# A second z buffer for the inverse transform, one piece of it to a slot, and a new order of work in the slots

## The chip, the cores and the metric

One core of a Trainium2 chip. The time is that of one execution on the device, in microseconds; lower is better. TensorE (PE) multiplies, ScalarE (ACT) and VectorE (DVE) empty its accumulators (PSUM) and do the elementwise work, GpSimd (POOL) issues some transfers, and the sync engine (SP) the others.

## What is computed

Eight sequences of 2496 rows of 256 numbers go through a spectral layer and then, row by row, through a mixture of eight experts with one expert to a row:

```python
X = np.fft.rfft(x, axis=1)
Yr = Xr @ w_r - Xi @ w_i + b_r
Yi = Xr @ w_i + Xi @ w_r + b_i
Yr = np.sign(Yr) * np.maximum(np.abs(Yr) - lam, 0.0)     # lam = 0.01, the same for Yi
y = np.fft.irfft(Y, n=x.shape[1], axis=1)
...
expert_idx = np.argmax(logits, axis=1)                    # logits = y @ w_gate, probs = softmax
for e in range(E):
    xe = y[mask]                                          # mask = expert_idx == e
    out[mask] = gate_w[mask, None] * (np.maximum(xe @ w1[e], 0.0) @ w2[e])
```

## The kernel before

The program has two long stages. The **spectral stage** handles eight batches (b) in ten slots (s) each, 80 slots in all; slot number `it` is 10 b + s. The **expert stage** multiplies 82 tiles of rows, sorted by expert, with the experts' weights.

Both transforms are done in two steps, as matmuls with fixed matrices. In the names of the program, which the profile shows too:

- `fwd_a` (matmul `pa`, copy `ae`) is the first step of the forward transform, for the next batch; its result goes to a buffer in DRAM (`spec`) and comes back transposed (`turn`, tile `t`).
- `fwd_b` (`pb`) is the second step, for the next slot. `halves` takes its result apart for a product in two parts: ScalarE copies `re` and `sh`, VectorE computes `su` and two `sl`.
- `mix` multiplies with the layer's weights: `pk` (copied to `k` by ScalarE) and `pm`, which VectorE adds to `k` as `v`.
- `shrink` is the soft threshold: `r` on ScalarE, four `y` on VectorE.
- `inv_b` (`pv`) is the first step of the inverse transform. ScalarE copies the result into the one large tile `z`, which holds a whole batch.
- `inv_a` is the second step. It needs the whole of `z`, and goes in twelve pieces: a piece has four matmuls `pz`, after each pair of which ScalarE rounds to `zh` and VectorE takes the rest `zl`, and six matmuls `py` on the `zh` and `zl` of the piece before, copied to `yb` by ScalarE.
- `route` is a generator that finds expert, gate and place of the finished rows: some 25 small steps, nearly all on VectorE (`lg`, `mx`, `scan`, `carry`, `carry_b`, `rb`), and the small matmuls `pr`. `tick(n)` takes n steps of the routes that are under way. `table` writes the list of tiles in the same manner, driven by `nudge`.

The order of the instructions on TensorE, ScalarE, VectorE and SP is that of the code; nothing reorders them. Tiles come from pools with a number of buffers; whoever takes a buffer again waits until its last reader is done. The accumulator tags are `u` (four buffers, for pa, pz, pv), `yo` (two, for pk, py and pr), and one buffer each for pb and pm.

Before the change there is one z. While batch b − 1 is taken out of it, slots of batch b cannot write to it, so their `inv_b` is put off: the twelve pieces stand in slots 2 to 5 of the next batch, three to a slot (`turning`), and the ten `inv_b` behind them, two to a slot from slot 6 on. After the last slot come the last two `inv_b` with eight warming matmuls (`keep_warm(8)`, `pw`) between them, the pieces of the last batch (`finish_last`), and the expert tiles, into whose first tiles the last routes' steps are laid by `breathe`.

Of the kernel before, what the change touches and what calls it, by code (L numbers as in the profile page):

```python
# [10 lines left out]
F32 = mybir.dt.float32  # L11
# [89 lines left out]
class Kernel:  # L101
    def __init__(self, tc, nb, x, w_r, w_i, b_r, b_i, w_gate, w1, w2,
                 c_fa, c_fe, c_ga, c_bm, c_bi, c_ids, c_score, c_base, c_ltri, c_tcol, out):
        self.__dict__.update({n: v for n, v in locals().items() if n != "self"})
        self.nc = tc.nc
        self.ntok = nb * S
        self.cap = TT + self.ntok
        self.nt = (self.ntok + E * (TT - 1)) // TT
        assert (nb - 3) * S - E * (TT - 1) > (EARLY - 1) * TT
        self.early = EARLY  # L110
        self.spec = [self.nc.dram_tensor(f"spec{i}_dram", (120, G, D), F32, kind="Internal").ap() for i in range(2)]
        self.xs = self.nc.dram_tensor("xs_dram", (E * self.cap, XW), F32, kind="Internal").ap()
# [24 lines left out]
    def open_inverse(self, st, pst):  # L137
# [34 lines left out]
        self.mark = k.tile([1, 1], F32, name="mark")  # L172
        self.z = k.tile([128, 2, 66, 40], F32, name="z")

    def open_forward(self, st):
        tc, nc, nb = self.tc, self.nc, self.nb
        f = self.f = self.pool(st, "f", 1, side="right")
        self.xst = ExitStack()
        self.xp = self.pool(self.xst, "xp", 5)
        self.tp = self.pool(st, "tp", 6, side="right")  # L180
# [15 lines left out]
        self.raw = {}  # L196
        self.braw = self.w.tile([33, 2, D], F32, tag="y", name="braw", bufs=6)
        for h, b in ((0, self.b_r), (1, self.b_i)):
# [12 lines left out]
        nc.gpsimd.dma_start(self.tcol, self.c_tcol)  # L211
        nc.gpsimd.memset(self.z[:, :, 64:66, :], 0.0)

# [38 lines left out]
    def split_bias(self):  # L252
        nc = self.nc
        zero = self.w.tile([128, 2, D], F32, tag="y", name="zero", bufs=6)
        nc.vector.memset(zero, 0.0)
        nc.vector.tensor_copy(self.bias, zero)
        nc.vector.tensor_scalar_add(self.ones, zero[:, 0, 0:128], 1.0)
        bh = self.w.tile([33, 2, D], F32R, tag="y", name="bh", bufs=6)
        nc.scalar.copy(self.bias[0:1], self.braw[0:1])
        nc.scalar.copy(bh[32:33], self.braw[32:33])  # L260
        nc.vector.tensor_sub(self.bias[32:33], self.braw[32:33], bh[32:33])
# [18 lines left out]
    def fwd_a(self, b, q, g):  # L280
# [4 lines left out]
                         self.xg[b, q][:m, g:g + 2, :].rearrange("p g d -> p (g d)"), start=True, stop=True)  # L285
        ae = self.xp.tile([120, 2, D], F32, tag="ae", name="ae", bufs=8)
        to = ae.rearrange("p g d -> p (g d)")
# [67 lines left out]
    def shrink(self, b, s):  # L355
# [4 lines left out]
        yield  # L360
        y = self.w.tile([128, 2, D], F32, tag="y", name="y", bufs=6)
        for kp in range(2):
# [8 lines left out]
    def inv_b(self, b, s):  # L371
        nc = self.nc
        y = self.ys.pop((b, s))
        p = self.psi.tile([128, 512], F32, tag="u", name="pv", bufs=4).rearrange(
            "p (c a r n) -> p c a r n", c=2, a=2, r=2)
        for kp in range(2):
            for c in range(2):
                nc.tensor.matmul(p[:, c, kp, :, :], y[:, kp, c * 128:(c + 1) * 128], self.bi[:, 2 * s + kp, :],  # L378
                                 start=True, stop=True)
        for c in range(2):  # L380
            nc.scalar.copy(self.z[:, c, 0:NB, 4 * s:4 * s + 4].rearrange("p n a -> p a n"),  # L381
                           p[:, c].rearrange("p a r n -> p (a r) n"))

    def inv_a(self, b, i):
        nc = self.nc
        for g in (2 * i, 2 * i + 1) if i < GH else ():
            p = self.psi.tile([128, 512], F32, tag="u", name="pz", bufs=4)
            for c in range(2):
                nc.tensor.matmul(p[:120, c * 136:(c + 1) * 136],  # L389
                                 self.z[:, c, 3 * g:3 * g + 3, :].rearrange("p j a -> p (j a)"), self.iw[:, c, :],  # L390
                                 start=True, stop=True)
# [16 lines left out]
    def spectral(self, fwd):  # L408
# [39 lines left out]
        for b in range(nb):  # L448
            for s in range(10):
                o = s + 2 if b == 0 or s > 7 else 6 + s // 2  # L450
                if 10 * b + o < n:
                    back[10 * b + o].append((b, s))

        for it in range(n):
            b, s = todo[it]
            half, small = iter(()), iter(())
            turning = b and 2 <= s < 6
            if it + 1 < n:
                self.fwd_b(*todo[it + 1])
                half = self.halves(*todo[it + 1])  # L460
                next(half)
            turns = iter(range(3 * s - 6, 3 * s - 3) if turning else ())

            def inverse():
                if back[it]:
                    self.inv_b(*back[it].pop(0))
                for i in turns:
                    self.inv_a(b - 1, i)
                    break

            if turning:
                inverse()
            if it:
                small = self.shrink(*todo[it - 1])
                next(small)
            next(half, None)
            self.tick(2)
            self.nudge(it)
            if not turning:
                inverse()  # L480
            mix = self.mix(b, s)
            if not turning:
                next(mix)
            for a in first[it]:
                self.fwd_a(*a)
            if turning:
                next(mix)
            next(small, None)
            self.tick(2)
            self.nudge(it)  # L490
            inverse()
            next(small, None)
            if it:
                self.pace(self.ys[todo[it - 1]][0:1, 1, 0:1])
                self.send(1)
            self.tick(1)
            next(mix, None)
            inverse()
            self.tick(1)
            self.pace(self.us[b, s][0:1, 0, 0:1])  # L500
            self.send(1)
            for a in loads[it]:
# [5 lines left out]
            if it + 4 < n:  # L508
                self.turn(*todo[it + 4])
            if b == nb - 2 and s == 1:  # L510
                self.tabling = self.table(0)
            if b == nb - 1 and s == 5:
                self.open_early()
        for _ in self.shrink(*todo[n - 1]):
            pass
        self.inv_b(*todo[n - 2])
        self.pace(self.ys[todo[n - 1]][0:1, 1, 0:1])
        self.send(1)
        self.keep_warm(8)
        self.inv_b(*todo[n - 1])  # L520
        self.pace(self.z[0:1, 1, 0, 36:37])
        self.send(1)
        fwd.close()

# [16 lines left out]

    def nudge(self, it=0):
        for _ in range(2 if it % 10 < 7 else 0):
            if next(self.tabling, "wait") == "wait":
                break

    def breathe(self):
        self.tick(3)
        self.nudge()

    def finish_last(self):
        tiles = itertools.chain.from_iterable(self.step(t) for t in range(BUSY))
        fill = itertools.chain(self.first1(), self.first2())
        for i in range(GH + 1):
            self.inv_a(self.nb - 1, i)
            if i:
                self.pace(self.yb[0:1, (2 * i - 1) % GH, 8:9])
                self.send(1)
            else:
                for _ in self.upright(0):  # L560
# [16 lines left out]
    def route(self, b, hf, y):  # L577
# [42 lines left out]
        nc.vector.tensor_copy(sb, pa[:, GH - 1, :])  # L620
        for _ in range(8 if b >= self.nb - 3 else 4):
            yield
# [388 lines left out]
```

## Time and profile before

| | |
|---|---|
| median of 3 runs | 1548.9 us (1548.7 to 1549.89) |
| profiled execution | 1556.04 us |
| its span, first to last instruction | 1554.3 us |
| TensorE busy | 1516.7 us, 98% |
| VectorE, ScalarE, GpSimd busy | 59%, 50%, 25% |

Busy times are those that the profiler records, and the ends of matmuls are modelled: a matmul's record is longer than the step to the next one. So 98% says that TensorE rarely has nothing to do, not that its array is at its peak. A matmul with fp32 operands is recorded as two. Starts are exact enough to measure steps between groups of matmuls, and a bracket at the end of a row of the timeline gives the engine's idle time before it and what ended it.

### The profile page before, as it was taken

What the parts mean: (1) busy time and instruction counts of PE and PEld (TensorE: products, weight loads), DVE (VectorE), ACT (ScalarE), POOL (GpSimd) and SP (SyncE); (2) the same over time, 40 slices, a digit from 0 to 9 for tenths busy, and PEclk for the clock granted to TensorE, in tenths of its full rate; (3) what the DMA queues carried; (4) which work ended last, traced back from release to release, by engine and by line L of the source; (5) the groups of instructions that cost most, each with busy time, mean ns of one, the idle gap of its engine ahead of it and who ended that gap; (6) DMA issues with size and microseconds to landing.
All of it is one profiled execution on the core that took longest, in us unless ns stands there. A gap on an engine that the chain in (4) does not pass through costs nothing. (4 is left out here: it accounts for less than half of the span.)

```text
span 1554.3 us, 35598 instructions
## 1 busy us (share of the span) xinstructions
PE 1516.7 (98%) x10934; PEld 1398.6 (90%) x10934; DVE 912.2 (59%) x2102; ACT 782.2 (50%) x1689; POOL 394.8 (25%) x554
## 2 busy tenths in 40 slices
PE   6999999999999999999999999999999999999997
PEld 3899999998989888889999999999999999999996
DVE  3677787777778777655455545545445445445442
ACT  2667777777767666344344434434334334334332
POOL 1002433425151534334311111111112111111111
PEclk7999999999999999999999999999999999999998
DMA  8864554646353422334234332323213213132210
GB/s 238 231 193 115 174 145 136 179 119 195 111 172 94 147 58 61 84 91 121 65 100 106 95 77 72 97 52 94 56 42 98 49 47 103 42 78 69 49 42 21
DMA packets 192834, 159.94 MB, mean 103 GB/s; under 512 B 127770, under 2 KB 163264, under 8 KB 192365
## 3 DMA queue, kind: packets, MB, share of 16 engines
q1 hardware_dynamic: 172685, 113.43, 28.8%
q0 software_dynamic: 19936, 44.04, 8.5%
q8 instruction: 89, 1.46, 0.4%
q14 instruction: 124, 1.02, 0.2%
HBM read 241.99 MB, written 66.37 MB: 198 GB/s over the span
## 5 line engine op out<-in xcount | busy, mean ns | idle before, releaser
L939 PE MATMUL po<-h,hh 128*128 128x512 f32 x1312 | 462.1, 395 | 0.0
L902 PE MATMUL ph<-xh,h 128*128 128x256 f32 x1312 | 372.0, 284 | 1.8 <-DVE hl L908 1.8
L902 PE MATMUL ph<-xl,h 128*128 128x256 f32 x1312 | 371.1, 283 | 0.0
L902 PE MATMUL ph<-xh,l 128*128 128x256 f32 x1312 | 370.7, 283 | 0.0
L936 PE MATMUL po<-h,hl 128*128 128x256 f32 x1148 | 324.0, 282 | 0.2 <-DVE hl L908 0.2
L908 DVE SCALAR_TENSOR_TENSOR hl<-ph,hh 128x512 fp32r<-128x512 f32 x328 | 226.2, 690 | 149.3 <-ACT hh L907 114.2
L907 ACT ACTIVATE hh<-ph 128x512 fp32r<-128x512 f32 x328 | 193.8, 597 | 204.0 <-PE ph L902 198.4
L939 PEld LDWEIGHTS po<-h,hh 128*128 128x128 f32 x1312 | 241.5, 188 | 43.8 <-issue 0.2
L948 POOL DMA_INDIRECT out<-o,row x124 | 123.8, 998 | 581.1 <-DVE o L946 472.7
L902 PEld LDWEIGHTS ph<-xh,l 128*128 128x128 f32 x1312 | 251.0, 191 | 3.7
L902 PEld LDWEIGHTS ph<-xh,h 128*128 128x128 f32 x1312 | 251.0, 191 | 3.2 <-DVE hl L908 3.2
L946 DVE SCALAR_TENSOR_TENSOR o<-po,xr,part 128x256 f32<-128x256 f32 x156 | 75.4, 484 | 302.6 <-ACTq L864 153.7
L902 PEld LDWEIGHTS ph<-xl,h 128*128 128x128 f32 x1312 | 251.1, 191 | 0.0
L945 ACT ACTIVATE part<-po,xr 128x256 f32<-128x256 f32 x156 | 73.8, 473 | 334.1 <-PE po L939 324.9
L936 PEld LDWEIGHTS po<-h,hl 128*128 128x128 f32 x1148 | 215.6, 188 | 6.3 <-DVE hl L908 2.1
L644 POOL DMA_INDIRECT xs_dram<-yb,pos x176 | 176.7, 1004 | 74.4 <-issue 63.8
L365 DVE SCALAR_TENSOR_TENSOR y<-v,r 64x256 f32<-64x256 f32 x320 | 134.0, 419 | 6.9 <-ACT r L359 0.8
L389 PE MATMUL pz<-iw,z 128*120 128x136 f32 x704 | 96.9, 280 | 2.5 <-DVE zl L395 1.7
L308 PE MATMUL pb<-bm,t 128*128 128x128 f32 x640 | 86.8, 279 | 12.3 <-DMA t<-spec_dram 9.5
L381 ACT COPY z<-pv 128x256 f32<-128x256 f32 x160 | 94.3, 712 | 5.9 <-PE pv L378 2.9
L308 PEld LDWEIGHTS pb<-bm,t 128*128 128x128 f32 x640 | 80.0, 195 | 13.5 <-issue 11.2
L389 PEld LDWEIGHTS pz<-iw,z 128*120 128x120 f32 x704 | 87.7, 183 | 3.5 <-DVE zl L395 1.9
(181 smaller groups left out, 2557.7 us busy)
## 6 DMA issues: line engine op xcount, KB each, us to landing
r<-moe_w SPq DMA_DIRECT2D x672, 128.0 KB
r<-moe_w SPq DMA_DIRECT2D x166, 512.0 KB
xq<-xs_dram SPq DMA_DIRECT2D x332, 64.0 KB
spec_dram<-ae SPq DMA_DIRECT2D x88, 240.0 KB
t<-spec_dram SPq DMA_DIRECT2D x160, 128.0 KB
x<-x SPq DMA_DIRECT2D x40, 384.0 KB
x<-x SPq DMA_DIRECT2D x40, 84.0 KB
xs_dram<-yb,pos POOLq DMA_INDIRECT x176
```

What stands on the lines that cost most here:

```text
L308: nc.tensor.matmul(p[:, c, :, kp, :], t[:, kp, c * 128:(c + 1) * 128], self.bm[:, 2 * s + kp, :], start=True, stop=True)
L365: nc.vector.scalar_tensor_tensor(out=y[q * 64:q * 64 + 64, kp, :], in0=u[h, q, :], scalar=LAM, in1=r[h, q, :], op0=ALU.add, op1=ALU.min)
L381: nc.scalar.copy(self.z[:, c, 0:NB, 4 * s:4 * s + 4].rearrange("p n a -> p a n"), p[:, c].rearrange("p a r n -> p (a r) n"))
L389: nc.tensor.matmul(p[:120, c * 136:(c + 1) * 136], self.z[:, c, 3 * g:3 * g + 3, :].rearrange("p j a -> p (j a)"), self.iw[:, c, :], start ...
L644: i = nc.gpsimd.indirect_dma_start(out=self.xs[:, :], out_offset=bass.IndirectOffsetOnAxis(ap=pos[:n, g:g + 1], axis=0), in_=y[:n, g, 0:XW ...
L902: nc.tensor.matmul(p[:, i, :], a[:, c, f * 128:(f + 1) * 128], v[:, c, :], start=m == 0, stop=m == 5)
L907: nc.scalar.activation(hh[:, s, :], p, AF.Relu)
L908: nc.vector.scalar_tensor_tensor(out=hl[:, s, :], in0=p, scalar=0.0, in1=hh[:, s, :], op0=ALU.max, op1=ALU.subtract)
L936: nc.tensor.matmul(p[:, :D], hl[:, f - 1, hs], w2[:, f - 1, 0, :], start=False, stop=False)
L939: nc.tensor.matmul(p, hh[:, f, hs], w2[:, f].rearrange("p a d -> p (a d)"), start=f == 0, stop=f == 7)
L946: nc.vector.scalar_tensor_tensor(out=o[:, h, :], in0=p[:, :D], scalar=xr[:, h, 0:1], in1=part, op0=ALU.mult, op1=ALU.add)
L948: i = nc.gpsimd.indirect_dma_start(out=self.out[:, :], out_offset=bass.IndirectOffsetOnAxis(ap=at[h], axis=0), in_=o[:, h, :], in_offset=N ...
```

## The change

There are two z buffers, and batch b uses z[b % 2]. `inv_b` of a slot now runs two slots later in every batch, right behind `fwd_b`, and its copies to z come later in the slot. The twelve pieces of batch b − 1 are spread over slots 2 to 11 of the next batch, one to a slot and two in slots 4 and 8 (slots 3 and 4 for batch 6, whose last three pieces stand behind the last slot). Within a slot ScalarE's order is re, sh, r, k, two z, sh, ae, two zh, two yb; VectorE's is su, sl, four y, sl, steps of a route, two zl, and v. A piece stands between `fwd_a` and the second half of `mix` (pm), a second piece at the slot's end. The waiting steps in front of pr are always eight, and the warming matmuls behind the last slot go. The pools of x, ae and y have fewer buffers, the table starts in slot 6 of batch 5 instead of slot 1 of batch 6, and of the issues that GpSimd makes (`pace`, `send`) one falls away in every other slot.

```diff
-        self.z = k.tile([128, 2, 66, 40], F32, name="z")
+        self.zs = [k.tile([128, 2, 66, 40], F32, name=f"z{i}") for i in range(2)]
...
-        self.xp = self.pool(self.xst, "xp", 5)
+        self.xp = self.pool(self.xst, "xp", 4)
...
-        ae = self.xp.tile([120, 2, D], F32, tag="ae", name="ae", bufs=8)
+        ae = self.xp.tile([120, 2, D], F32, tag="ae", name="ae", bufs=6)
...
-        y = self.w.tile([128, 2, D], F32, tag="y", name="y", bufs=6)
+        y = self.w.tile([128, 2, D], F32, tag="y", name="y", bufs=3)
...
+        yield
         for c in range(2):
-            nc.scalar.copy(self.z[:, c, 0:NB, 4 * s:4 * s + 4].rearrange("p n a -> p a n"),
+            nc.scalar.copy(self.zs[b % 2][:, c, 0:NB, 4 * s:4 * s + 4].rearrange("p n a -> p a n"),
...
-                o = s + 2 if b == 0 or s > 7 else 6 + s // 2
-                if 10 * b + o < n:
-                    back[10 * b + o].append((b, s))
+                if 10 * b + s + 2 < n:
+                    back[10 * b + s + 2] = (b, s)
+        pieces = {i: [] for i in range(n)}
+        for b in range(nb - 1):
+            for i, o in enumerate((2, 3, 3, 4, 4, 5, 6, 7, 8) if b == nb - 2 else (2, 3, 4, 4, 5, 6, 7, 8, 8, 9, 10, 11)):
+                pieces[10 * b + 10 + o].append((b, i))
...
-            half, small = iter(()), iter(())
-            turning = b and 2 <= s < 6
+            half, small, turned = iter(()), iter(()), iter(())
+            self.tick(2)
             if it + 1 < n:
                 self.fwd_b(*todo[it + 1])
                 half = self.halves(*todo[it + 1])
                 next(half)
-            turns = iter(range(3 * s - 6, 3 * s - 3) if turning else ())
-
-            def inverse():
-                if back[it]:
-                    self.inv_b(*back[it].pop(0))
-                for i in turns:
-                    self.inv_a(b - 1, i)
-                    break
-
-            if turning:
-                inverse()
+            if back[it]:
+                turned = self.inv_b(*back[it])
+                next(turned)
             if it:
                 small = self.shrink(*todo[it - 1])
                 next(small)
-            next(half, None)
-            self.tick(2)
-            self.nudge(it)
-            if not turning:
-                inverse()
             mix = self.mix(b, s)
-            if not turning:
-                next(mix)
-            for a in first[it]:
-                self.fwd_a(*a)
-            if turning:
-                next(mix)
-            next(small, None)
-            self.tick(2)
-            self.nudge(it)
-            inverse()
-            next(small, None)
+            next(mix)
+            for _ in itertools.chain(turned, small, half):
+                pass
             if it:
                 self.pace(self.ys[todo[it - 1]][0:1, 1, 0:1])
                 self.send(1)
+            for a in first[it]:
+                self.fwd_a(*a)
             self.tick(1)
+            for a in pieces[it][:1]:
+                self.inv_a(*a)
+            self.tick(4 if it > n - 4 else 2)
+            self.nudge()
             next(mix, None)
-            inverse()
             self.tick(1)
-            self.pace(self.us[b, s][0:1, 0, 0:1])
-            self.send(1)
+            self.nudge()
+            if s % 2 or b >= nb - 2:
+                self.pace(self.us[b, s][0:1, 0, 0:1])
+                self.send(1)
+            for a in pieces[it][1:]:
+                self.inv_a(*a)
...
-            if b == nb - 2 and s == 1:
+            if b == nb - 3 and s == 6:
                 self.tabling = self.table(0)
...
-        for _ in self.shrink(*todo[n - 1]):
+        small = self.shrink(*todo[n - 1])
+        next(small)
+        for _ in self.inv_b(*todo[n - 2]):
             pass
-        self.inv_b(*todo[n - 2])
+        for i in (9, 10):
+            self.inv_a(nb - 2, i)
+            next(small, None)
...
-        self.keep_warm(8)
-        self.inv_b(*todo[n - 1])
-        self.pace(self.z[0:1, 1, 0, 36:37])
+        for _ in self.inv_b(*todo[n - 1]):
+            pass
+        self.tick(2)
+        self.inv_a(nb - 2, 11)
...
     def breathe(self):
-        self.tick(3)
-        self.nudge()
+        self.tick(4)
...
-        for _ in range(8 if b >= self.nb - 3 else 4):
+        for _ in range(8):
             yield
         p = self.psi.tile([128, 512], F32, tag="yo", name="pr")
```

TensorE before, in a slot in which a route reaches `pr`: the small matmuls stand behind pv and ahead of pm, in a slot that has no piece of the inverse.

```order
L284 MATMUL pa<-x,far 120x512
L378 MATMUL pv<-bi,y 128x128 x4
L624 LDWEIGHTS ltri
L624 MATMUL pr<-sb,ltri 117x8
L625 LDWEIGHTS ones_b
L625 MATMUL pr<-carry_b,ones_b 117x8
L335 MATMUL pm<-bias,ones 128x256
```

TensorE after, in slot 24: the end of the slot before, then pb of this one.

```order
L623 LDWEIGHTS ltri
L623 MATMUL pr<-sb,ltri 117x8
L624 LDWEIGHTS ones_b
L624 MATMUL pr<-carry_b,ones_b 117x8
L309 MATMUL pb<-bm,t_2088 128x2x64 x4
L379 MATMUL pv<-bi,y 128x128 x4
L339 MATMUL pk<-whr,sh 128x256
```

And further on in the same slot, behind pk:

```order
L339 MATMUL pk<-whr,sl 128x256
L285 MATMUL pa<-x,far 120x512
L391 MATMUL pz<-iw,z_108 120x136 x4
L405 MATMUL py<-zh,gh 117x272
L405 MATMUL py<-zh,gl 117x272
L405 MATMUL py<-zl,gh 117x272
L405 MATMUL py<-zh,gh 117x272
L405 MATMUL py<-zh,gl 117x272
```

So pr moved to the end of a slot, and pk and a pair of py now follow it, on the same accumulator tag.

VectorE before, behind the same pr: rb, its reader, stands behind four y, v and carry_b.

```order
L365 SCALAR_TENSOR_TENSOR y<-v,r 64x256 x4
L626 TENSOR_TENSOR carry<-carry,scan_102 117x8
L352 TENSOR_TENSOR v<-pm,k 128x512
L628 CAST carry_b<-carry 117x8
L630 SCALAR_TENSOR_TENSOR rb<-pr,base 117x8
L321 TENSOR_TENSOR su<-re,pb 128x256
L322 TENSOR_TENSOR sl<-pb,sh 128x2x256
L325 TENSOR_TENSOR sl<-su,sh 128x2x128
```

VectorE after, in slot 24: v is that of the slot before.

```order
L353 TENSOR_TENSOR v<-pm,k 128x512
L625 TENSOR_TENSOR carry<-carry,scan_102 117x8
L322 TENSOR_TENSOR su<-re,pb 128x256
L323 TENSOR_TENSOR sl<-pb,sh 128x2x256
L366 SCALAR_TENSOR_TENSOR y<-v,r 64x256 x4
L326 TENSOR_TENSOR sl<-su,sh 128x2x128
L627 CAST carry_b<-carry 117x8
L629 SCALAR_TENSOR_TENSOR rb<-pr,base 117x8
L397 TENSOR_TENSOR zl<-pz,zh 120x272 x2
```

So rb now stands behind all of a slot's su, sl and y, and ahead of the slot's zl.

TensorE before, between the last slot's last pv and the last batch's pieces, from the last warming matmul on:

```order
L528 MATMUL pw<-idle 128x512
L378 MATMUL pv<-bi,y 128x128 x4
L389 MATMUL pz<-iw,z 120x136 x4
L624 LDWEIGHTS ltri
L624 MATMUL pr<-sb,ltri 117x8
L625 LDWEIGHTS ones_b
L625 MATMUL pr<-carry_b,ones_b 117x8
L389 MATMUL pz<-iw,z 120x136 x4
L403 MATMUL py<-zh,gh 117x272
```

TensorE after, behind the last pm of the last slot, where pieces of batch 6 (z_107) begin:

```order
L339 MATMUL pm<-whs,sl 128x256
L379 MATMUL pv<-bi,y 128x128 x4
L391 MATMUL pz<-iw,z_107 120x136 x4
L405 MATMUL py<-zh,gh 117x272
L405 MATMUL py<-zh,gl 117x272
L405 MATMUL py<-zl,gh 117x272
L405 MATMUL py<-zh,gh 117x272
```

And from the last pv to the first piece of the last batch (z_108):

```order
L379 MATMUL pv<-bi,y 128x128 x4
L405 MATMUL py<-zh,gh 117x272
L405 MATMUL py<-zh,gl 117x272
L405 MATMUL py<-zl,gh 117x272
L405 MATMUL py<-zh,gh 117x272
L405 MATMUL py<-zh,gl 117x272
L405 MATMUL py<-zl,gh 117x272
L391 MATMUL pz<-iw,z_108 120x136 x8
```

So two pieces of batch 6 now stand behind the last pm, and one pair of its py between the last pv and the last batch's first pz, where warming matmuls stood ahead of that pv.

## Rows read from the trace of the kernel before

**Rows 1.** Windows: length, busy PE, PEld, DVE, ACT, POOL, granted clock, DMA share, GB/s
```profile
24.00:40.00 16.00, 7.49 (x33) 7.26 (x34) 5.39 (x10) 4.04 (x9) 0.00 (x0) 0.50 0.79 245
40.00:440.00 400.00, 399.21 (x3054) 364.99 (x3053) 298.98 (x816) 291.88 (x711) 124.34 (x210) 1.00 0.56 160
440.00:566.00 126.00, 121.48 (x969) 114.42 (x969) 98.49 (x292) 87.38 (x221) 44.11 (x72) 1.00 0.42 118
565.97:591.57 25.60, 21.26 (x158) 18.46 (x157) 19.43 (x56) 17.03 (x39) 13.98 (x24) 1.00 0.18 54
591.57:690.00 98.43, 96.39 (x685) 89.04 (x684) 61.28 (x168) 44.35 (x97) 37.60 (x52) 1.00 0.31 82
690.00:1544.00 854.00, 852.83 (x5999) 797.68 (x5997) 422.04 (x743) 330.86 (x606) 166.35 (x177) 1.00 0.29 72
```

**Rows 2.** Waits of TensorE: total us, times, longest us
```profile
PE pb L308 <- DMA t<-spec_dram: 9.5, 1, 9.5
PE py L403 <- ACT yb L404: 2.2, 1, 2.2
...
PE ph L902 <- DVE hl L908: 1.8, 2, 1.4
PE pz L389 <- DVE zl L395: 1.7, 1, 1.7
```

**Rows 3.** Timeline of TensorE, one slot: start us, duration us, then the instructions
```profile
304.71 1.05 PE L308 MATMUL pb<-bm,t 128*128 128x128 f32 x8
305.60 1.06 PE L378 MATMUL pv<-bi,y 128*128 128x128 f32 x8
306.41 0.36 PE L338 MATMUL pk<-whr,sh 128*128 128x256 f32 x1
...
307.21 1.02 PE L284 MATMUL pa<-x,far 117*120 117x512 f32 x2
...
309.73 1.05 PE L308 MATMUL pb<-bm,t 128*128 128x128 f32 x8
```

**Rows 4.** Timeline of VectorE, the same slot
```profile
306.75 0.42 DVE L321 TENSOR_TENSOR su<-re,pb 128x256 f32<-128x256 f32 x1 [1.05 <-ACT re L319]
...
307.69 0.41 DVE L325 TENSOR_TENSOR sl<-su,sh 128x256 fp32r<-128x256 f32 x1
308.02 1.73 DVE L365 SCALAR_TENSOR_TENSOR y<-v,r 64x256 f32<-64x256 f32 x4
```

**Rows 5.** Timeline of VectorE, a slot in which a route goes on
```profile
514.09 0.19 DVE L628 CAST carry_b<-carry 117x8 bf16<-117x8 f32 x1
514.19 0.15 DVE L630 SCALAR_TENSOR_TENSOR rb<-pr,base 117x8 f32<-117x8 f32 x1
```

**Rows 6.** Timeline of ScalarE, a slot with pieces of the inverse
```profile
311.62 0.69 ACT L394 CAST zh<-pz 120x272 fp32r<-120x272 f32 x2
...
316.11 0.39 ACT L404 COPY yb<-py 117x272 f32<-117x272 f32 x1 [0.34 <-issue]
```

**Rows 7.** Timeline of TensorE, from the last slot to the first expert tile
```profile
578.07 1.89 PE L528 MATMUL pw<-idle 128*128 128x512 bf16 x8
...
583.54 0.17 PE L624 MATMUL pr<-sb,ltri 117*117 117x8 bf16 x1
...
584.54 0.37 PE L403 MATMUL py<-zh,gh 120*117 120x272 f32 x1
...
587.32 0.38 PE L403 MATMUL py<-zh,gh 120*117 120x272 f32 x1 [2.16 <-ACT yb L404]
...
587.79 1.09 PE L389 MATMUL pz<-iw,z 128*120 128x136 f32 x8
588.62 0.39 PE L403 MATMUL py<-zh,gh 120*117 120x272 f32 x1
...
589.49 1.09 PE L389 MATMUL pz<-iw,z 128*120 128x136 f32 x8
```

**Rows 8.** Timeline of the sync engine's queue at the start
```profile
4.47 6.36 SPq L277 DMA_DIRECT2D x<-x  x8
```

More of the change, by code (lines that the diff above doesn't have):

```diff
@@ L108, in __init__ @@
         self.nt = (self.ntok + E * (TT - 1)) // TT
-        assert (nb - 3) * S - E * (TT - 1) > (EARLY - 1) * TT
+        assert (nb - 4) * S - E * (TT - 1) > (EARLY - 1) * TT
         self.early = EARLY
@@ L196, in open_forward @@
         self.raw = {}
-        self.braw = self.w.tile([33, 2, D], F32, tag="y", name="braw", bufs=6)
+        self.braw = self.w.tile([33, 2, D], F32, tag="y", name="braw", bufs=3)
         for h, b in ((0, self.b_r), (1, self.b_i)):
@@ L211, in open_forward @@
         nc.gpsimd.dma_start(self.tcol, self.c_tcol)
-        nc.gpsimd.memset(self.z[:, :, 64:66, :], 0.0)
+        for z in self.zs:
+            nc.gpsimd.memset(z[:, :, 64:66, :], 0.0)
     def load_w(self, nm):
@@ L253, in split_bias @@
         nc = self.nc
-        zero = self.w.tile([128, 2, D], F32, tag="y", name="zero", bufs=6)
+        zero = self.w.tile([128, 2, D], F32, tag="y", name="zero", bufs=3)
         nc.vector.memset(zero, 0.0)
@@ L257, in split_bias @@
         nc.vector.tensor_scalar_add(self.ones, zero[:, 0, 0:128], 1.0)
-        bh = self.w.tile([33, 2, D], F32R, tag="y", name="bh", bufs=6)
+        bh = self.w.tile([33, 2, D], F32R, tag="y", name="bh", bufs=3)
         nc.scalar.copy(self.bias[0:1], self.braw[0:1])
@@ L389, in inv_a @@
                 nc.tensor.matmul(p[:120, c * 136:(c + 1) * 136],
-                                 self.z[:, c, 3 * g:3 * g + 3, :].rearrange("p j a -> p (j a)"), self.iw[:, c, :],
+                                 self.zs[b % 2][:, c, 3 * g:3 * g + 3, :].rearrange("p j a -> p (j a)"), self.iw[:, c, :],
                                  start=True, stop=True)
@@ L513, in spectral @@
                 self.open_early()
-        for _ in self.shrink(*todo[n - 1]):
-            pass
-        self.inv_b(*todo[n - 2])
+        small = self.shrink(*todo[n - 1])
+        next(small)
+        for _ in self.inv_b(*todo[n - 2]):
+            pass
+        for i in (9, 10):
+            self.inv_a(nb - 2, i)
+            next(small, None)
         self.pace(self.ys[todo[n - 1]][0:1, 1, 0:1])
         self.send(1)
-        self.keep_warm(8)
-        self.inv_b(*todo[n - 1])
-        self.pace(self.z[0:1, 1, 0, 36:37])
+        for _ in self.inv_b(*todo[n - 1]):
+            pass
+        self.tick(2)
+        self.inv_a(nb - 2, 11)
+        self.pace(self.yb[0:1, GH - 1, 8:9])
         self.send(1)
+        self.tick(2)
         fwd.close()
@@ L540, in send, with nudge @@
                 n -= 1
[L542 to L545, printed above, removed]
+    def nudge(self):
+        next(self.tabling, None)
     def breathe(self):
-        self.tick(3)
-        self.nudge()
+        self.tick(4)
     def finish_last(self):
@@ L557, in finish_last @@
                 self.pace(self.yb[0:1, (2 * i - 1) % GH, 8:9])
+                self.send(2 if i == 3 else 1)
+            else:
+                self.pace(self.hl[1][0].bitcast(F32)[0:1, 0:1])
                 self.send(1)
-            else:
                 for _ in self.upright(0):
```

## The prediction

> **What bounds the kernel now.** I read the times first, then the windows, because one share over the whole span hides stages with different limits. [rows 1] gives five stages that matter here. From 40 to 440 us TensorE is busy 399.21 of 400.00 us, and in the expert tiles from 690 us 852.83 of 854.00. Time is to be had only where TensorE is not busy: 400.00 − 399.21 = 0.79 us up to 440 and 126.00 − 121.48 = 4.52 up to 566, together 5.31; 4.3 us of 25.60 at the boundary (565.97 to 591.57, where 1.89 of the busy time is only warming, [rows 7]); 2.0 us in the first tiles up to 690; and the head, where the first spectrum waits 9.5 us for a transfer [rows 2]. Next the waits of TensorE [rows 2]: apart from the head's they are single ones, on a copy or a subtraction that ScalarE or VectorE did late. The longest from ScalarE is 2.2 us, from VectorE 1.7. Then the timeline of one steady slot [rows 3]: each group of matmuls starts as the last one's issue ends. The order among them is therefore free: the same matmuls in another order take the same time, as long as their inputs are there. VectorE and ScalarE matter only where TensorE comes to them too early.
>
> **The change, part by part.** The matmuls of the slots stay the same in kind and number; eight warming ones go. So the sum consists of waits that go and waits that come. I make it against the profiled execution's own 1556.04 us (span 1554.3); that one is 7.1 us above the median of 1548.9, so I carry only the difference over to the median.
>
> (a) *One piece of the inverse per slot instead of up to three.* Slots 2 to 5 of a batch held three pieces and all copies for them; now most slots hold one. If none of the waits of 40 to 566 us comes back, 5.31 us go. A recorded idle time is too short, though: ends are modelled, and eight pb take 1.05 us in the record while pv starts 0.89 us after them [rows 3], 0.16 us earlier. With some eight places of idle time that is 8 × 0.16 = 1.3, so at most 6.6 us. Below, nothing goes if VectorE is late again in other slots: two of every ten slots now have two pieces, and the table's steps start five slots earlier, on top of routing. I take 5.6, one of the longer waits coming back in the slots of batch 5 that are fullest on VectorE. Bounds 0 and 6.6.
>
> (b) *The boundary.* Before, 25.60 us hold these matmuls, by counts from the order of the program and steps from rows: pb 4 (0.89), pv 24 (6 × 0.81), pk 12 (2 × 0.80) [rows 3]; pm 28 (2 × 1.66, which is the slot's 309.73 − 304.71 = 5.02 less 0.89, 0.81, 0.80 and 0.86 for one pa, the last an estimate by 1.02 − 0.16); pz 16 (4 × 0.83) and py 18 (3 × 0.87) [rows 7]. Sum 16.6, so 9.0 us are lost, the 1.89 of warming among them. After, the same stretch holds pz 28, py 42 and pv 16 (pieces that stood earlier now stand here, and two pv groups less): 0.89 + 3.24 + 1.60 + 3.32 + 5.81 + 6.09 = 21.0 us of work. What is still lost in it is the chain of the last slot (v, r, y, pv, z, then pz) less the two pieces and the pair of py now laid over it, and the first pieces of the last batch, whose zl stands on VectorE behind the expert weights' and tokens' splits. The 9.0 is the upper bound if nothing is hidden; taking the eight warming matmuls and nothing else away gives 7.1. I take 7: a gain of 2.0, bounds 0 and 4.
>
> (c) *The first expert tiles.* Rows of the sort that cost now (ph waits 1.8 us on hl) stay. New is that in two of these tiles the pr matmuls stand right ahead of a pair of py. Both tags share two accumulator buffers, so while pr is unread the pair has one, and its second py waits for ScalarE's copy of the first. The trace has this once: pr at 583.5, first py at 584.54, second at 587.32 after 2.16 us idle on yb [rows 7]. There ScalarE was full of other splits. In a tile it costs at least the copy (0.39, [rows 6]) with the way there and back, less nothing, since nothing stands between: I take 0.7 each, and 0.9 for denser steps on VectorE between two hl: 2.3. Bounds 0.8 and 4.4.
>
> (d) *The wait that the change adds.* The eight steps of waiting in a route now always pass, and 6 steps run per slot, so pr of a route lands at the end of a slot, twice in ten slots, 12 times in all. Behind it come pb, pv, pk, pa, pz, and now a pair of py, which before never followed a pr in these slots. pr, pk, py, py need four buffers of a tag that has two. So the second py waits until rb has read pr, and rb stands on VectorE behind su, sl, four y, sl2 and carry_b of the slot. From [rows 4]: su starts 306.75 − 304.71 = 2.04 us after pb, what follows sl starts 0.94 after su (307.69 − 306.75), sl2 takes 0.33 (308.02 − 307.69) and the four y 1.73. In the new order: 2.04 + 0.94 + 1.73 + 0.33 = 5.04. carry_b and rb: 0.10 to rb's start and 0.15 for it [rows 5], 5.29, and with the signal about 5.37. The second py would come at 0.89 + 0.81 + 0.80 (pb, pv, pk) + 0.86 for each pa + 0.83 (pz) + 0.43 (first py). With two pa that is 5.48, no wait; with one 4.62, so 0.75, and 0.10 to refill: 0.85. Two pa stand in slots 20, 30, 40, 50 and 60, one in 24, 34, 44, 54 and 64: 5 × 0.85 = 4.25. In slots 70 and 74 there is no pa, and the buffers fall as in (c): the second py waits for the first's copy, which stands behind two zh (0.69, then 0.39, [rows 6]): 0.1 + 0.69 + 0.39 + 0.1 less 0.43 = 0.9 each, 1.8. Sum 6.05. Bounds: 0 if rb runs 0.8 us earlier than I placed it, and 12 × 0.9 = 10.8.
>
> The Trainium skill says that the same gap repeating on the engine that should be saturated can mean too little PSUM for the next tile (page "Perfetto Trace Analysis", section "Optimization Strategy"). The trace of before has such a gap only once, the 2.16 us at 587.32, and agrees there; by this rule the buffers of py, not VectorE's speed, would have to be blamed for (d).
>
> (e) *Eight warming matmuls less, and the clock.* The granted clock is 0.50 from 24 to 40 us, after TensorE had idled 9.5 us, and 1.00 from then on, through the boundary with its 2.2 us gap [rows 1, 2]. With gaps no longer than that the clock should stay. I cost it at nothing; the price otherwise is among the rivals.
>
> The Trainium skill's rule is to leave no idle gaps between bursts of matmuls, lest the clock fall to half (page "TensorE: Matmul & The Clock Gate", section "Why this matters for your kernels"). That speaks against dropping the warming; the trace shows a fall only behind the 9.5 us, none behind 2.2.
>
> (f) *Smaller pools.* Four x buffers for five, six ae for eight, three y for six. The eight x issues of the head take 6.36 us [rows 8], so a load held back until a buffer is free starts about 2 us later; the wait behind it is for a chain of transfers that is full anyway (DMA share 0.79 there), so 0, bounds 0 and 2. y lives two slots, so three are enough; ae is read by a transfer within a slot or two. ScalarE's and VectorE's new order inside a slot costs nothing in steady slots: y ends 0.02 us after the next pb in [rows 3, 4] and pv reads it a slot later.
>
> Sum: −5.6 − 2.0 + 2.3 + 6.05 = +0.75 us.
>
> **The rivals.**
> *Trade, as above* (0.44): 1549.6, between 1546 and 1552.
> *The wait on rb does not bite* (0.27). If VectorE reaches rb 0.8 us earlier (v done before pb starts, su not held by ScalarE), or the pairs of py come late for another reason, (d) is 0 and the rest stands: −5.3, 1543.6; half of it gives 1546. For it: sl2 and rb are short, and ScalarE takes re and sh first. Against it: v starts 0.3 us after pb in [rows 3, 4], and nothing in the slot starts it sooner.
> *Slower by VectorE's queue* (0.23). Route steps ahead of v push v, then su, y and rb. Each 0.4 us in the 12 slots with pr costs 4.8 us, and VectorE's lateness also brings (a)'s waits back, first the one of 1.7 us on zl. With 0.4 us: +5.5, 1554.4. It decides from 0.2 us per slot on. For it: rb is the eighth instruction behind pb. Against it: VectorE is busy 299 of 400 us, three quarters.
> *The clock falls* (0.03). If the boundary's gaps let the clock fall to half (1.2 GHz) for a stretch as long as in the head, 16.00 us, half of it is lost: +8 to the sum, 1557.7.
> *Nothing happens, since TensorE was full anyway* (0.03): 1548.9. The idle 5.31 us and the new buffers speak against it.
>
> **How the numbers follow.** The 0.2% that a measurement of this kernel can tell from no change are 3.1 us: below 1545.8 is faster, above 1552.0 slower. The trade holds mostly inside, with 0.04 on either side; of the rb case I put 0.24 below and the rest inside. Faster 0.28, same 0.44, slower 0.28. The likeliest case's own range is 1546 to 1552; with the two next to it, to their centres and a little less than 0.1 out on each side, 1543.5 to 1554.8.
>
> **What would show it.** In the waits after: py on rb, about five times 0.7 us, in one-pa slots with pr; two of 0.9 on yb in slots 70 and 74; the waits of pz on zl and pk on yb gone; idle time between 40 and 566 us near 6 us; from slot 78's pb to the first ph about 28 us; granted clock 1.00 there. I am wrong if TensorE's idle time up to 566 is below 2 us (rb on time), if pm waits for v or pv for y in many slots (VectorE late), or if the expert tiles change by more than 4 us.

## The result, and the profile after

The changed kernel takes 1561.45 us (median, 1560.82 to 1561.84), the one before 1549.22 in the same set of runs: a ratio of 1.0077, interval 1.0064 to 1.0091. It is 12.2 us slower; 0.7 us had been forecast, and a range that ended at 1554.8.

The two profiles first shown lie only 5.6 us apart (spans 1559.9 and 1554.3), because that of before, from which [rows 1 to 8] come, was a long execution. A second profile of before has a span of 1547.0, and is the one to compare with. The next fence has its windows, up to the last slot, the boundary to the first expert matmul, and the tiles to 690 us (columns as in [rows 1]):

```profile
40.00:440.00 400.00, 400.00 (x3065) 366.19 (x3065) 299.53 (x818) 292.25 (x714) 126.09 (x213) 1.00 0.56 161
440.00:559.14 119.14, 118.01 (x955) 112.46 (x954) 97.75 (x291) 86.77 (x219) 43.12 (x70) 1.00 0.43 121
559.14:584.75 25.61, 21.21 (x157) 18.46 (x157) 19.43 (x56) 17.04 (x39) 14.00 (x24) 1.00 0.18 54
584.75:690.00 105.25, 103.57 (x740) 96.11 (x739) 65.64 (x175) 47.77 (x102) 40.14 (x57) 1.00 0.32 83
```

And the same stretches of the changed kernel, with the expert tiles behind 690:

```profile
40.00:440.00 400.00, 397.31 (x3027) 361.98 (x3026) 295.58 (x793) 284.77 (x704) 112.88 (x190) 1.00 0.56 157
440.00:563.57 123.57, 118.79 (x965) 113.01 (x965) 98.39 (x297) 86.12 (x218) 50.73 (x89) 1.00 0.42 122
563.57:592.82 29.25, 23.36 (x182) 21.50 (x181) 21.86 (x68) 19.43 (x50) 13.28 (x22) 1.00 0.26 65
592.82:690.00 97.18, 91.62 (x655) 84.31 (x654) 61.48 (x173) 43.23 (x92) 35.64 (x49) 1.00 0.31 82
690.00:1544.00 854.00, 854.00 (x6005) 798.84 (x6004) 426.69 (x751) 334.56 (x614) 171.37 (x185) 1.00 0.30 75
```

In this execution of before, as long as the median ones, TensorE idles 0.00 + 1.13 us in the slots from 40 us on, and not the 5.31 of [rows 1]. In the changed one it idles 2.69 + 4.78. In the tiles up to 690 us it is 1.68 against 5.56. Behind 690 us nothing differs. The changed kernel's waits of TensorE say on what, to set beside [rows 2]:

```profile
PE pb L309 <- DMA t<-spec_dram: 9.5, 1, 9.5
PE py L405 <- ACT yb L406: 6.3, 6, 1.4
PE ph L901 <- DVE hl L907: 4.0, 4, 1.4
PE py L405 <- DVE rb L629: 2.6, 5, 0.5
PE py L405 <- DVE zl L397: 2.2, 2, 1.4
...
PE pr L623 <- ACT yb L406: 1.3, 1, 1.3
PE pv L379 <- DVE y L366: 0.9, 1, 0.9
PE pn L678 <- ACT yb L406: 0.6, 1, 0.6
```

Five waits of py on rb, and a single wait on yb that has become six, five of them behind a pr or a pq: these small matmuls now stand among py pairs. One of the five is slot 24 of the changed kernel, TensorE's timeline first, then VectorE's:

```profile
183.17 1.14 PE L309 MATMUL pb<-bm,t 128*128 128x128 f32 x8
...
186.61 1.09 PE L391 MATMUL pz<-iw,z 128*120 128x136 f32 x8
187.45 0.38 PE L405 MATMUL py<-zh,gh 120*117 120x272 f32 x1
...
188.60 0.38 PE L405 MATMUL py<-zh,gh 120*117 120x272 f32 x1 [0.52 <-DVE rb L629]
```

```profile
185.29 0.42 DVE L322 TENSOR_TENSOR su<-re,pb 128x256 f32<-128x256 f32 x1 [0.82 <-ACT sh L321]
...
186.23 1.73 DVE L366 SCALAR_TENSOR_TENSOR y<-v,r 64x256 f32<-64x256 f32 x4
187.97 0.43 DVE L326 TENSOR_TENSOR sl<-su,sh 128x256 fp32r<-128x256 f32 x1
...
188.38 0.16 DVE L629 SCALAR_TENSOR_TENSOR rb<-pr,base 117x8 f32<-117x8 f32 x1
```

rb starts 5.21 us behind pb; 5.14 had been worked out. The second py starts 5.43 behind it, where without the wait it would come at 4.75 (0.47 us behind the first py, as in the run with seven steps below).

The table has the length of the stages in us, each worked out as a difference of starts in the timelines: slot 10's pb, the last pb, the first ph, and the first hl of tile 45.

| stage | before, 2nd profile | changed | 7 steps | 3 per breath | both edits |
|---|---|---|---|---|---|
| head and slots 0 to 9 | 88.6 | 89.9 | 88.6 | 88.1 | 87.1 |
| slots 10 to the last pb | 470.6 | 473.6 | 466.2 | 473.6 | 466.2 |
| boundary, to the first ph | 25.6 | 29.2 | 29.7 | 28.9 | 28.5 |
| tiles 0 to 44 | 532.4 | 537.2 | 541.9 | 534.5 | 534.1 |
| the rest | 429.9 | 429.9 | 429.8 | 430.1 | 430.0 |

The last three columns are the next section's. By (b) of the prediction 4.4 us of work move from the slots to the boundary (21.0 against 16.6). So the slots lost 473.6 − 470.6 + 4.4 = 7.4 us to waits, the boundary gained 0.8, the tiles lost 4.8, and the head and the first slots 1.3. The last is not the change's: a second profile of the changed kernel (below) has 88.6 us there, as before.

### The profile page after: what moved, and what is told of

Its sections match the earlier page's. It is cut to its first block, busy times and chain, and to the rows that moved or that the text cites. A ratio compares the mean times of both kernels' runs of the same rounds, so it can differ in the third digit from the quotient of the medians.

```text
span 1559.9 us, 35552 instructions
## 1 busy us (share of the span) xinstructions
PE 1515.1 (97%) x10926; PEld 1396.7 (90%) x10926; DVE 917.4 (59%) x2110; ACT 779.7 (50%) x1697; POOL 393.5 (25%) x555
## 3 DMA queue, kind: packets, MB, share of 16 engines
q1 hardware_dynamic: 174125, 115.53, 28.9%
## 5 line engine op out<-in xcount | busy, mean ns | idle before, releaser
L947 POOL DMA_INDIRECT out<-o,row x124 | 123.2, 994 | 581.7 <-DVE o L945 473.6
L643 POOL DMA_INDIRECT xs_dram<-yb,pos x176 | 180.5, 1026 | 87.4 <-issue 79.7
L391 PEld LDWEIGHTS pz<-iw,z 128*120 128x120 f32 x704 | 90.9, 183 | 25.4 <-issue 22.8
```

The lines of the kernel that those rows point to most:

```text
L391: nc.tensor.matmul(p[:120, c * 136:(c + 1) * 136], self.zs[b % 2][:, c, 3 * g:3 * g + 3, :].rearrange("p j a -> p (j a)"), self.iw[:, c, : ...
L643: i = nc.gpsimd.indirect_dma_start(out=self.xs[:, :], out_offset=bass.IndirectOffsetOnAxis(ap=pos[:n, g:g + 1], axis=0), in_=y[:n, g, 0:XW ...
L947: i = nc.gpsimd.indirect_dma_start(out=self.out[:, :], out_offset=bass.IndirectOffsetOnAxis(ap=at[h], axis=0), in_=o[:, h, :], in_offset=N ...
```

## The experiments

Theory A: py waits, since two accumulators and a late rb hold it up. Theory B: the first tiles, since the route's steps stand denser ahead of hl. A third possibility was that the first profile of before did not show where it usually spends its time.

**Before, unchanged, a second profile.**

> The kernel before, unchanged, for a second profile. The first one was 7.1 us over the median of its runs, and only 5.6 us under the changed kernel's profile, while the medians lie 12.2 us apart. If that execution was a long one, this one ends near 1549 us, and the stage that is now some 7 us shorter shows where the missing 6.6 us of the difference are. If profiling itself costs before 7 us, it ends near 1556 again with the same stages.

Median 1549.38, ratio 0.9997 (0.9988 to 1.0007), the profiled execution 1548.83. The long execution's 7 us lay in the slots: 5.6 us from slot 58 to the last, in slots 62, 72 and 73 above all (10.85, 8.47 and 10.43 us, against 8.50, 7.61 and 8.69). So most of what (a) meant to win does not occur in the executions whose median was forecast.

**rb ahead of su: seven waiting steps.**

```diff
-        for _ in range(8):
+        for _ in range(7):
             yield
         p = self.psi.tile([128, 512], F32, tag="yo", name="pr")
```

> The changed kernel with seven waiting steps ahead of pr for eight: pr and its reader rb fall into the same pair of steps, so rb stands ahead of su on VectorE. Theory A (py waits because rb stands behind su, sl and y): the five waits of 0.7 us on rb go, and those of 1.5 us on yb behind an unread pr where the pair has one buffer; 4 to 8 us faster than the changed kernel, so 1553 to 1557. Theory B (the loss lies in the first expert tiles and the boundary): within 2 us of 1561.

1557.6, 3.9 us under the changed kernel (ratio to before 1.0041, 1.0029 to 1.0054), and just beyond the range of theory A. In slot 24 now, on TensorE and on VectorE:

```profile
186.12 0.38 PE L405 MATMUL py<-zh,gh 120*117 120x272 f32 x1
...
186.59 0.29 PE L405 MATMUL py<-zh,gh 120*117 120x272 f32 x1
```

```profile
182.97 0.16 DVE L629 SCALAR_TENSOR_TENSOR rb<-pr,base 117x8 f32<-117x8 f32 x1
183.96 0.42 DVE L322 TENSOR_TENSOR su<-re,pb 128x256 f32<-128x256 f32 x1 [0.83 <-ACT sh L321]
```

No wait, and VectorE lost nothing: it waits for ScalarE ahead of su anyway. The slots from 10 on got 7.4 us shorter: slots 24, 34, 44, 54 and 64 fell from 9.24 to 8.45, slot 70 from 7.53 to 5.92, slot 74 from 9.20 to 7.57. In the slots that is theory A in full. The total gave back half of it: the tiles got 4.7 us longer, since in one of them pr now waits 1.8 us for sb on VectorE, and in two stretches the granted clock fell:

```profile
580.00:590.00 10.00, 8.70 (x46) 8.14 (x47) 8.05 (x25) 5.91 (x16) 4.52 (x6) 0.66 0.30 75
...
620.00:630.00 10.00, 8.25 (x42) 7.12 (x42) 5.23 (x21) 1.54 (x3) 1.01 (x1) 0.83 0.09 20
```

Not every execution has that fall: two of the six took 1554.6 and 1555.0 us at a mean granted clock of 0.993, the other four, the profiled one among them, 1557.3 to 1558.3 at 0.989.

**Three steps per breath, as before.**

```diff
     def breathe(self):
-        self.tick(4)
+        self.tick(3)
```

> The changed kernel with three steps of a route per breath in the first expert tiles, as before, for four. Theory B: ph waits for hl because the four steps stand ahead of it on VectorE; the tiles from 592 to 690 us get 2 to 4 us shorter, 1557 to 1559. Theory A: within 1 us of 1561, since the waits there come from pr and py.

1558.15, 3.3 us under the changed kernel (1.0051, 1.0035 to 1.0068). The tiles fell from 537.2 to 534.5 us, the slots stayed at 473.6. Theory B holds a part too. What is left of the waits on hl:

```profile
PE ph L901 <- DVE hl L907: 1.6, 1, 1.6
```

**Both edits.**

> The changed kernel with both edits, seven waiting steps and three steps per breath. If A and B each hold a part and they are independent, the gains of the two single runs add up; if the missing 6.6 us of before's profile are a loss elsewhere, even this stays 4 us or more above 1549.

1549.71, ratio to before 1.0001 (0.9991 to 1.0010). Together they give back 11.7 us, 4.6 more than the single gains' sum of 7.2: with three steps per breath pr of the first tiles no longer comes before its sb, the granted clock stays at 1.00 in the profile, and the tiles take 534.1 us and not 541.9. The two causes are shown, and that they are not independent. How much of the 4.6 us is pr's wait and how much the clock is an estimate: against the two executions of seven steps at 0.993, 1.8 us are left over, as much as pr waited for sb.

**pr on the other accumulators.** In the sets of runs from here on before takes 1557 to 1558 us, so ratios to before are compared, not times.

```diff
-        p = self.psi.tile([128, 512], F32, tag="yo", name="pr")
+        p = self.psi.tile([128, 512], F32, tag="u", name="pr", bufs=4)
```

> The changed kernel with pr's accumulator taken from the four buffers of pa, pz and pv instead of the two of pk and py; the order on every engine stays. Theory A1 (too few accumulator buffers make py wait; VectorE is early enough for anybody who takes the buffer later): the waits of py on rb and of py on yb behind pr go, the slots from 90 to 562 us get some 6 us shorter, pz or pv of later work wait for nothing, total 1554 to 1556. Theory A2 (VectorE is late as a whole): the wait only moves, to pz or pv, and the total stays within 2 us of 1561.

1559.59, where before took 1558.06: 1.0005 (0.9992 to 1.0017). The changed kernel itself is at 1.0037 on another chip on which before takes 1557.4 (below). If the two chips may be compared, this wins 0.3%, some 5 us, without moving an instruction in any queue. The waits on rb are gone; a part has moved:

```profile
PE py L405 <- ACT yb L406: 1.3, 1, 1.3
PE pz L391 <- ACT z L383: 1.3, 5, 0.3
```

Slot 24 takes 8.96 us (9.24 with the wait, 8.45 without). So slots 24, 34, 44, 54 and 64 won back 0.28 us or less of their 0.79, because a pz in them now waits for ScalarE's copy to z. Slots 20, 30, 40, 50 and 60, which have two pa, got 0.28 to 0.35 us longer than in the changed kernel, so these ten together won nothing. Slots 70 and 74 are as short as with both edits, 1.6 us each. For those two A1 holds, and in the other ten the shortage went to the tag with four, which has no buffer to spare there either. A2 does not hold: pz waits for ScalarE, not for VectorE. The slots from 10 on take 471.4 us, for 473.6 and 477.1 in the two profiles of the changed kernel; some 6 us less had been expected.

The Trainium skill's rule on a gap that repeats (page "Perfetto Trace Analysis", section "Optimization Strategy") names too little PSUM as a possible cause; this trace agrees, with 0.52 us five times, though moving rb in its queue cured it wholly, and the tag with more buffers only in part.

**The table's steps one nudge later, on top of both edits.**

```diff
-        for _ in range(6 if last else 0):
+        for _ in range(6 if last else 1):
             yield "wait"
```

> Changed kernel with seven waiting steps and three steps per breath, and the table's steps one nudge later, so that its matmul pq and the reader of pq fall into one slot. If the single waits of 1.5 us (py behind pq) and 0.75 us (pn behind py) come from pq and pn standing between py pairs on the two buffers, the first goes: 1.5 us faster than the 1549.7 of the kernel with the two edits. If they are VectorE's table steps as such, no change.

1552.73, ratio 0.9972 (0.9962 to 0.9983), where both edits have 0.9969 on another chip of this kind (below): no gain. Slot 57 got 0.8 us shorter, as pn no longer waits in it. pq moved from the end of slot 67 into slot 68: the one got 1.1 us shorter, the other 1.3 longer (10.48 for 9.21). There pq itself now waits 1.0 us and the py behind it 0.5, where that py alone had waited 1.4, so pq's wait did not go.

**The eight warming matmuls back, on top of both edits.**

> Changed kernel with seven waiting steps and three steps per breath, and the eight warming matmuls back between the last two pv. If dropping them costs clock, the boundary has a granted clock under 1.00 without them and this one is faster; if not, it is 0 to 1.9 us slower than 1549.7, as much as isn't laid over the wait for y.

1552.53, 0.9965 (0.9955 to 0.9976): neither a loss nor a gain that can be told from 0.9969. The granted clock of the boundary is 1.00 in the profiles with and without the warming matmuls, so here there was nothing for them to keep up.

**pr on the four, three steps per breath, the table later.**

> Changed kernel with pr in the four-buffer tag (eight waiting steps), three steps per breath and the table one nudge later. If the accumulators of py are the whole loss in the slots and the denser steps that of the tiles, 1547 to 1549, at or just under the kernel before. If pulling the two apart brought the kernel with both edits back only by its shift of a step, 1552 or more.

1553.79, 0.9972 (0.9962 to 0.9983). By its ratio it lies under before, as with both edits, and the intervals cannot tell the two apart; its expected 1547 to 1549 us were those of a chip on which before takes 1549. In the slots it is not as good: slots 20 and 24 are again the longer ones (7.98 and 8.96 us, for 7.64 and 8.45).

**The changed kernel again, on such a chip.**

> The changed kernel again, on the same chip as the next three. The runs so far were on two kinds of chip: one on which the kernel before takes 1549, one on which it takes 1558, and the profile shown of before (1556) has the longer slots of the second kind. If the waits of (a) belong to such a chip alone, the changed kernel is 0.7 to 0.8% slower where before takes 1549, and 0.1 to 0.4% slower where it takes 1556 to 1558. If the ratio is the same everywhere, 1.0077 again.

1563.97 where before took 1557.4: 1.0037 (1.0025 to 1.0050), and 1.0077 in the first set. So part of before's extra time on this chip goes with the change, as forecast. That it is the waits (a) meant is not shown, since no profile of before was taken there. The changed kernel has extra time on it too: 141.8 us from slot 58 to the last pb, against 138.3 in its first profile.

**Seven steps with the warming matmuls.**

> The changed kernel with seven waiting steps, and the eight warming matmuls back. With seven steps alone the profile has a granted clock of 0.66 and 0.83 in two stretches of 10 us between 580 and 630 us, the tiles there are 5 us longer, and the runs lie in two groups (1554.6 to 1555.0, 1557.3 to 1558.3). If the clock is what parts them, the warming keeps it at 1.00, the tiles shrink to those of the kernel with both edits but for the four steps, and all runs lie near the lower group. If the tiles are long for another reason (routes a step earlier), the groups and the long tiles stay.

1558.12, 1.0002 (0.9992 to 1.0012). The theory that the warming keeps the clock up falls. Of this kernel:

```profile
580.00:590.00 10.00, 7.91 (x50) 7.26 (x49) 9.26 (x27) 8.58 (x23) 4.67 (x7) 0.83 0.16 49
620.00:630.00 10.00, 8.20 (x44) 7.02 (x43) 5.95 (x24) 1.07 (x2) 0.97 (x1) 0.83 0.00 0
```

The tile there is as long as without the warming (17.2 us, against 12.6 with both edits). Ahead of the second fall stand a wait of ph on hl (1.15 us) and one of pr on sb (1.80 us), ahead of the first the waits of py on yb and zl in the boundary. One burst of matmuls ahead of another stretch of waits did not help here. That the clock parts the executions is not refuted: of these twelve the shortest (1555.81 us) had a mean granted clock of 0.994, the longest (1560.58) one of 0.989.

**Both edits again.**

> The changed kernel with seven waiting steps and three steps per breath again, for comparison on one chip with the others: 11 to 12 us under the changed kernel, as on the first chip, if the two edits hold whatever the chip. Against before: equal where before takes 1549, 0.3% faster where it takes 1556 or more.

1552.86, 0.9969 (0.9957 to 0.9981): 11.1 us under the changed kernel on this chip too.

**All small matmuls off the two buffers.** Seven steps, three per breath, warming, and pr, pn and pq in the four-buffer tag:

```diff
-        p = self.psi.tile([128, 512], F32, tag="yo", name="pn")
+        p = self.psi.tile([128, 512], F32, tag="u", name="pn", bufs=4)
...
-        p = self.psi.tile([128, 512], F32, tag="yo", name="pq")
+        p = self.psi.tile([128, 512], F32, tag="u", name="pq", bufs=4)
```

> The changed kernel with seven waiting steps, three steps per breath, the warming matmuls back, and pr, pn and pq on the accumulators of pa, pz and pv, so that no small matmul stands between pk and py on two buffers. The waits left in the slots (0.75 on pn, 1.5 on pq, 1.5 on pr of the last slots) go if they are a matter of those two buffers: 2 to 4 us under the kernel with both edits. If VectorE's lateness is behind them, they move to pz, and the time stays.

1547.78, where before took 1557.4 and the kernel with both edits 1552.86: 0.9935 (0.9918 to 0.9951). It is 5.1 us under both edits, for 2 to 4 expected, and beats both kernels on this chip; on a chip of the first sort it was not run. From 440 us to the last pb TensorE has 0.3 us of idle time, and of the waits on yb one is left, in the boundary:

```profile
440.00:552.01 112.01, 111.71 (x922) 107.76 (x922) 93.54 (x281) 80.70 (x208) 51.79 (x87) 1.00 0.46 129
```

```profile
PE py L405 <- ACT yb L406: 1.3, 1, 1.3
```

## Why the prediction was wrong

- **The step that failed is (a).** Its waits were read from one execution that was 7.1 us longer than the median, and then set off against the median, in whose executions they are all but absent (1.13 us for 5.31). Without that −5.6 the same sum is +6.35, and the forecast 1555; by the table, whose two profiles lie 12.9 us apart, the rest of the miss is 2.5 us in (c), 1.4 in (d), 1.2 in (b) and 1.3 in the head. The warning stood in the text, as "I carry only the difference over"; but waits that an execution has beyond the median are not there to be won. With (d)'s waits taken out by the seven steps the slots take 466.2 us, with the 4.4 moved to the boundary 470.6, as before: (a) won nothing beyond what the new waits of pn and pq (0.6 and 1.4 us) took back. Its mechanism was not right for the long execution either. The longest of its waits, TensorE's on zl, was put down to pieces that crowd VectorE; but VectorE was late there because it had itself waited 3.44 us for TensorE:

```profile
453.85 0.69 DVE L352 TENSOR_TENSOR v<-pm,k 128x512 f32<-128x512 f32 x1 [3.44 <-PE pa L284]
```

```profile
456.22 0.72 PE L389 MATMUL pz<-iw,z 128*120 128x136 f32 x4 [1.71 <-DVE zl L395]
```

- **(d) was right in mechanism and place**, and for 6.05 us measured 7.4. The five slots cost 0.79 each, for 0.85; slot 30, put at nothing, cost 0.2. The 0.08 us for the signal and the 0.10 to refill stand in no row; the second py starts 0.06 us behind the end of rb. Slots 70 and 74 cost 1.6 each, for 0.9: ahead of yb on ScalarE there stand not only the two zh but also two z and sh. ScalarE's timeline of slot 70 of the changed kernel, where py's first copy is the last row:

```profile
513.96 0.37 ACT L345 COPY k<-pk 128x256 f32<-128x256 f32 x1
514.23 1.17 ACT L383 COPY z<-pv 128x256 f32<-128x256 f32 x2
515.16 0.45 ACT L325 CAST sh<-su 128x256 fp32r<-128x256 f32 x1
515.49 0.69 ACT L396 CAST zh<-pz 120x272 fp32r<-120x272 f32 x2
516.04 0.43 ACT L406 COPY yb<-py 117x272 f32<-117x272 f32 x1
```

- **(c) was mis-sized**: 4.8 us for 2.3, beyond its upper bound of 4.4 and the 4 us that the prediction named as a sign of being wrong. The two waits of py behind pr are there, with 0.47 us each. The denser steps, put at 0.9, were worth 2.7 by themselves, 537.2 − 534.5, and more together with pr's place, in part by the granted clock.
- **(b)** gained 0.8 us, not 2.0: the first pieces of the last batch wait for yb (1.3 us) and zl (0.8 and 1.4), and a pr in slot 78 waits 1.3 us for yb.
- **(e)** was wrong that the clock stays, and right, as far as these runs can tell, that the warming is worth nothing. In the first profile of the changed kernel it stays at 1.00; in that of its second run it fell, by the window from 590 us, and the first tile took 29.4 us for 27.9, the boundary 29.8 for 29.2:

```profile
590.00:600.00 10.00, 8.58 (x45) 7.87 (x44) 8.16 (x24) 6.41 (x17) 4.73 (x7) 0.66 0.21 55
```

  The rival had priced it at 8 us; it is some 2. The reading behind (e) was wrong too: in before the clock does not fall behind the 9.5 us of idle time, which last from 20.96 to 30.45 us, but inside them:

```profile
22.00:24.00 2.00, 0.00 (x0) 0.00 (x0) 0.80 (x2) 0.46 (x1) 0.00 (x0) 0.75 0.99 356
```

  And with seven steps it fell in the boundary behind waits of 0.9, 1.3 and 0.8 us, each shorter than the 2.2 us behind which it stayed at 1.00. So the longest gap of before was no bound to go by.
- **The rival on the other side** named VectorE's queue ahead of rb, and put 1554.4 on it. The place was right, but rb was not late beyond the trade's own estimate (5.21 us for 5.14); what was missing was that there was nothing to set it off against.
- **(f)** and the free order inside the slots held as far as the runs show: with both edits the kernel with the smaller pools and the new order is at 1.0001 of before. No run changes the pools alone. Slots from 11 on without a route's or the table's small matmuls have the same length to some 0.02 us in all twelve profiles of the changed order, but for slots 63 and 73, which differ even between two profiles of the same program (6.78 and 8.51 us for slot 63).

## What to carry to other kernels

Waits that are to be removed must be there in the execution that counts: if the profiled one is longer than the median by more than the expected gain, take a second profile ahead of any sum. Look for matmuls of a few columns, such as pr, that take an accumulator from a tag with two buffers, and for their reader's place in its engine's queue; moving the reader ahead of one slot's work gave back all of the slots' loss, moving the tile to a tag with more buffers only a part, because that tag had no buffer to spare in most of these slots. Steps laid between other work by number (eight waits, four per breath) interact: undo them one by one and together.

## What the runs showed that was not expected

- The same program took different times in different sets of runs: before 1549 us in the first two and 1557 to 1558 in the last two, both edits 1549.7 and 1552.9. The three sets of experiments were taken on one chip each; that the chip is the reason, and that the long profile of before was of such a chip, is likely but not shown. In the long profile of before the difference lies mostly in the slots from 58 on, where VectorE and ScalarE wait for matmuls that TensorE's records show as done some 3 us earlier: v starts at 453.85, though the last pm ahead of it is recorded at 450.27. Why, stays open; TensorE's records don't show it.
- The granted clock fell at the boundary or in the first tiles in seven of the twelve profiles of kernels with the changed order (0.66 to 0.96 by window of 10 us, 0.50 at its lowest), with the warming matmuls too, and in neither profile of before, whose gap of 2.2 us there is the longest single one. What sets it off stays open.
- A recorded wait understates its cost: the wait on rb is recorded as 0.52 us, and costs the slot 0.79.
